# Router logits of an attention + mixture-of-experts kernel: token strips turned by VectorE instead of TensorE transposes, and two products instead of eight for the counts

## The chip, the cores and the metric

One core of one Trainium2 chip. The metric is the device time of one execution in microseconds, the median of 3 runs; lower is better.

## What is computed

Sigmoid attention on 8 batches x 12 heads x 448 tokens x 64, its output read as 3584 tokens x 768, and a mixture of experts on top of it, in which a token takes part only when its skip score is positive, and then with one expert:

```python
scores = scale * np.matmul(q, k.transpose(0, 1, 3, 2)) - np.log(S)
x = np.matmul(1.0 / (1.0 + np.exp(-scores)), v)      # rearranged to (3584, 768)
do_compute = x @ w_skip > 0
logits = x[do_compute] @ w_gate                        # 8 experts
e_idx = argmax(logits);  gate_w = softmax(logits)[e_idx]
y[e_idx == e] = gate_w * (relu(x @ w1[e]) @ w2[e])     # w1: 768x1024, w2: 1024x768
out = x.copy();  out[do_compute] = x + y
```

## The kernel before, in words

**Attention** runs as 48 steps `n`, one for each batch `b` and pair of heads `hp` (6 pairs in a batch), in an order written out by hand (`tc.manual_schedule`, the loop at line 692). A step has four parts `c` of keys (parts 0 to 2 with 448 queries, part 3 with 224). For each part TensorE makes scores (`scores`, L223, tile `s`), ScalarE takes the sigmoid (L243, tile `at`), and TensorE multiplies with the values two parts later (`values`, L251, tile `pa`). Keys and queries are loaded by SP two steps ahead, partly copied by GpSimd (L173) and turned by VectorE (L191). The finished rows of a pair are kept in `xt` (L689 on ScalarE, L261 on VectorE), turned (L266, tile `y`) and stored.

All tiles of scores share two PSUM slots, which alternate:

```python
def new_s(name):
    turn[0] ^= 1
    return ps_s.tile([P, 2, 512], F32, tag=f"s{turn[0]}", name=name)
```

`new_t`, from which the tiles of the router come, takes the next of the same two slots during attention. A tile in a slot is free when its last reader is done, and the scores two places later wait for that.

**Routing of batch b-1 lies inside the steps of batch b.** `xt` holds the 768 features on partitions, in six blocks `i` of 128, and the 448 tokens on columns.

- hp 0, part 3: `logits` (L291) multiplies each block with 32 weight columns (8 gates, the skip vector, zeros) in one of four column groups of TensorE: blocks 0 to 3 with all 448 tokens, one per group, blocks 4 and 5 in two halves of 224 tokens. The four groups hold partial sums. `keep_logits` (L302) copies all of it, 128x448, out of PSUM on VectorE (tile `lt`).
- hp 1, part 2: `turn_logits` turns `lt` by four TensorE transposes of 112 tokens (L308, tile `pg`, a slot of its own) and VectorE adds the four partial sums (L312, tile `lg`). `route` then finds the expert: `mx`, `d`, `first`, `fm`, `hot`, and `hb`, a one for the chosen expert of each token (L322 to L356).
- hp 2: `gates` (L376 to L382), and in part 3 `route_count`: each token's place in its expert's list is a count of earlier tokens of that expert. With the token's chunk of 112 on columns and the token within it on partitions, this takes one product with a triangle (L388), three with ones for the chunks before (L390) and four that sum all chunks for the running `base` (L398), all into `pc`, again in a slot. VectorE reads it (L406 to L420: `pos`, `base`, `sel`, `idx`).
- Four indirect DMAs on GpSimd (L425) put the records into the experts' lists.

The last batch does this after the loop (lines 840 to 886), between the products of the first expert block (`gemm1`, L527; `gemm2`, L555): `logits` with `parts=4`, where blocks 4 and 5 go in four pieces of 112 tokens. From step 22 on SP also loads weights of the first expert (tile `wr`), which VectorE and GpSimd split (L496, L497). After that a loop over blocks of tokens (L1558) does the rest; where few rows are left (`few`, L1403), its products have 32 weight columns and 128 moving columns in four column groups (L1409).

In the profile every product of float32 operands stands as two records, one for each half of its weights.

Of the kernel before, what the change touches and what calls it, by code (L numbers as in the profile page):

```python
# [10 lines left out]
F32 = mybir.dt.float32  # L11
F32R = mybir.dt.float32r
BF16 = mybir.dt.bfloat16
I32 = mybir.dt.int32
# [5 lines left out]
P = 128  # L20
# [3 lines left out]
def kernel(  # L24
# [62 lines left out]
    ones = const.tile([CP, P], BF16, name="ones")  # L87
    nc.vector.memset(ones, 1.0)

# [3 lines left out]
    nc.gpsimd.iota(tok_i, pattern=[[CP, NC]], base=0, channel_multiplier=1)  # L93
# [185 lines left out]
    def col(c):  # L279

        return slice(c * CP, (c + 1) * CP)
# [17 lines left out]

    def keep_logits(b, pl):  # L300
        lt = io.tile([P, S], F32, tag="wr", name=f"lt_{b}", bufs=WB)
        nc.vector.tensor_copy(lt, pl[:, :S])  # L302
        return lt

    def turn_logits(b, lt):
        pg = new_t(f"pg_{b}")
        for c in range(NC):
            nc.tensor.transpose(  # L308
                pg[:CP, c * P : (c + 1) * P], lt[:, col(c)], ident
            )  # L310
        lg = sm.tile([CP, NC, NE + 1], F32, tag="lg", name=f"lg_{b}", bufs=1)
        nc.vector.tensor_reduce(  # L312
            lg,
            pg[:CP, :].rearrange("p (c g e) -> p c e g", c=NC, g=4)[:, :, : NE + 1, :],
            axis=AX.X,
            op=ALU.add,
        )
        return lg

    def route(b, lg):  # L320
        mx = sm.tile([CP, NC], F32, tag="mx", name=f"mx_{b}", bufs=1)
        nc.vector.tensor_reduce(mx, lg[:, :, :NE], axis=AX.X, op=ALU.max)  # L322
        rec = sm.tile([CP, NC, REC], F32, tag="rec", name=f"rec_{b}")
        nc.gpsimd.memset(rec, 0.0)
        nc.gpsimd.tensor_scalar(
            rec[:, :, 1], tok[:CP], float(b * S), None, op0=ALU.add
        )
        d = sm.tile([CP, NC, NE], F32, tag="d", name=f"d_{b}", bufs=1)
# [3 lines left out]
            mx.unsqueeze(2).to_broadcast([CP, NC, NE]),  # L332
# [3 lines left out]
        first = sm.tile([CP, NC, NE], F32, tag="first", name=f"first_{b}", bufs=1)  # L336
# [4 lines left out]
            desc[:CP].unsqueeze(1).to_broadcast([CP, NC, NE]),  # L341
# [3 lines left out]
        fm = sm.tile([CP, NC], F32, tag="fm", name=f"fm_{b}", bufs=1)  # L345
        nc.vector.tensor_reduce(fm, first, axis=AX.X, op=ALU.max)
        hot = sm.tile([CP, NC, NE], F32, tag="hot", name=f"hot_{b}", bufs=1)
# [3 lines left out]
            fm.unsqueeze(2).to_broadcast([CP, NC, NE]),  # L351
# [3 lines left out]
        hb = sm.tile([CP, NC, NE], BF16, tag="hb", name=f"hb_{b}", bufs=1)  # L355
        nc.vector.scalar_tensor_tensor(  # L356
            hb,
            lg[:, :, NE : NE + 1].to_broadcast([CP, NC, NE]),
# [4 lines left out]
        )  # L363
        return rec, hb, d

    def weigh_route(b, rt):

        sg = sm.tile([CP, NC, NE], F32, tag="sg", name=f"sg_{b}", bufs=1)
# [3 lines left out]
    def gates(b, rt):  # L372
        rec, sg = rt[0], sgs[b]

        om = sm.tile([CP, NC, NE], F32, tag="om", name=f"om_{b}", bufs=1)
# [3 lines left out]
        sume = sm.tile([CP, NC], F32, tag="sume", name=f"sume_{b}", bufs=1)  # L379
# [4 lines left out]
    def route_count(b, rec, hb):  # L384
# [1206 lines left out]
```

## Time and profile before

| | us |
|---|---|
| median of 3 runs (lowest, highest) | 521.59 (521.33, 522.76) |
| the profiled execution | 520.3 |
| its span, first to last instruction | 518.5 |
| TensorE busy in the span | 505.6 (98%) |
| VectorE, ScalarE, GpSimd busy | 294.2, 279.2, 239.8 |
| attention (up to the last scores) | about 279 of the span |
| granted TensorE clock, mean | 0.993 |

The profiled execution is 1.3 us under the median, and 1.8 us of it lie outside the span. The records of TensorE overlap in time (four groups work at once), so what a piece of its work costs is read from where the next piece starts, not from the length of its records.

### The profile page before, as it was taken

How to read it: one execution, taken by the hardware profiler on the slowest of the kernel's cores; microseconds unless marked ns; L12 is line 12 of the kernel's file. 1: busy time of each engine (PE TensorE's matmuls, PEld its weight loads, DVE VectorE, ACT ScalarE, POOL GpSimd, SP SyncE). 2: the span in 40 equal slices, each digit the busy share in tenths (PEclk: the TensorE clock that was granted, in tenths of full speed). 3: DMA queues.
4: the chain of work that ended last, by engine and by line, in shares of the span. 5: the costliest groups of instructions: out<-in, count | busy, mean ns of one | idle time of the engine just before them, and what ended most of it. 6: DMA issues, size and time to landing. Idle time of an engine off the chain costs nothing.

```text
span 518.5 us, 15420 instructions
## 1 busy us (share of the span) xinstructions
PE 505.6 (98%) x5037; PEld 342.8 (66%) x5038; DVE 294.2 (57%) x696; ACT 279.2 (54%) x481; POOL 239.8 (46%) x355
## 2 busy tenths in 40 slices
PE   8999999999999999999999999999999999999991
PEld 6885555555545555555455889957769797979790
DVE  4546856658578678775695862681222332349522
ACT  5776786767767766677676212761122323258321
POOL 4523454443457676765675402332321434344634
PEclk9999999999999999999999999999999999999997
DMA  8998877897999999989975106949395879796943
GB/s 206 207 250 190 186 170 156 174 174 173 202 194 234 223 206 216 200 192 228 195 157 118 20 32 199 383 124 363 105 350 191 269 286 296 262 329 243 348 177 47
DMA packets 142081, 107.22 MB, mean 207 GB/s; under 512 B 99163, under 2 KB 114523, under 8 KB 142032
## 3 DMA queue, kind: packets, MB, share of 16 engines
q1 hardware_dynamic: 133792, 96.11, 71.3%
q0 software_dynamic: 4032, 8.51, 6.7%
q10 hardware_dynamic: 4208, 1.95, 1.5%
q8 instruction: 30, 0.49, 0.4%
q14 instruction: 19, 0.16, 0.1%
HBM read 98.49 MB, written 17.56 MB: 224 GB/s over the span
## 4 chain that ended last, share of the span: by engine, by line
PE 93%; DVE 2%; DMA 1%; issue 1%; POOL 1%; SPq 1%; ACT 0%; POOLq 0%; ACTq 0%; DVEq 0%
PE s L223 24%; PE pa L251 23%; PE ph L527 11%; PE py L555 11%; PE b_ph L527 3%; PE b_py L555 3%; PE ph L1409 3%; PE py L1409 2%; PE py L1478 2%; PE ph L1478 2%; PE pxt L503 2%; PE pl L291 2%; PE pht L541 1%; PE pg L308 1%; DMA kq<-in_k_dram 1%
## 5 line engine op out<-in xcount | busy, mean ns | idle before, releaser
L243 ACT ACTIVATE at<-s,bias 128x896 f32<-128x896 f32 (+1 forms) x191 | 174.0, 914 | 79.6 <-PE s L223 68.8
L251 PE MATMUL pa<-at,v 64*64 64x448 f32 (+1 forms) x1536 | 168.3, 489 | 0.0
L223 PE MATMUL s<-x 64*64 64x448 f32 (+1 forms) x1504 | 166.7, 496 | 0.4 <-DVE sel L418 0.4
L173 POOL COPY kq<-kq 32x896 f32<-32x896 f32 (+1 forms) x96 | 87.9, 915 | 96.2 <-DMA kq<-in_q_dram 55.8
L223 PEld LDWEIGHTS s<-x 64*64 64x64 f32 x1504 | 82.6, 191 | 47.9 <-issue 25.4
L251 PEld LDWEIGHTS pa<-at,v 64*64 64x64 f32 x1536 | 65.8, 133 | 54.6 <-issue 45.6
L191 DVE STREAM_TRANSPOSE x<-kq 128x448 f32<-128x448 f32 x94 | 80.7, 931 | 4.7 <-POOL kq L173 4.7
L261 DVE TENSOR_TENSOR xt<-xt,pa 128x448 f32<-128x448 f32 x48 | 29.7, 619 | 50.8 <-ACT xt L689 50.8
L425 POOL DMA_INDIRECT lst<-rec,idx x32 | 31.6, 988 | 16.3 <-issue 5.3
L497 POOL TENSOR_TENSOR wl<-wr,wh 128x384 fp32r<-128x384 f32 (+1 forms) x28 | 31.5, 1136 | 11.1 <-DVE wh L496 7.6
L266 DVE STREAM_TRANSPOSE y<-xt 128x448 f32<-128x448 f32 x48 | 31.0, 645 | 7.8 <-DMA out_dram<-y 6.3
L547 DVE TENSOR_TENSOR hl<-pht,hh 128x512 fp32r<-128x512 f32 x14 | 9.7, 689 | 41.4 <-ACT hh L546 41.4
L536 ACT ACTIVATE hs<-ph 128x512 f32<-128x512 f32 x14 | 8.4, 599 | 42.1 <-PE ph L527 26.3
L585 POOL DMA_INDIRECT out_dram<-ys,rp x15 | 22.8, 1519 | 16.3 <-POOLq L1558 8.4
L555 PE MATMUL py<-wh,hh 128*128 128x384 f32 x112 | 29.8, 347 | 0.0
L555 PE MATMUL py<-wh,hl 128*128 128x384 f32 x112 | 28.8, 338 | 0.0
L555 PE MATMUL py<-wl,hh 128*128 128x384 f32 x112 | 28.7, 337 | 0.0
L513 DVE TENSOR_TENSOR xl<-pxt,xh 128x384 fp32r<-128x384 f32 x30 | 15.3, 551 | 20.8 <-ACT xf L1108 20.3
L527 PE MATMUL ph<-wl,xh 128*128 128x512 f32 x84 | 26.3, 400 | 0.0
L689 ACT ACTIVATE xt<-pa 128x448 f32<-128x448 f32 x48 | 25.7, 536 | 0.8 <-PE pa L251 0.8
L527 PE MATMUL ph<-wh,xh 128*128 128x512 f32 x84 | 25.4, 399 | 0.0
L527 PE MATMUL ph<-wh,xl 128*128 128x512 f32 x84 | 24.1, 391 | 0.0
(268 smaller groups left out, 657.0 us busy)
## 6 DMA issues: line engine op xcount, KB each, us to landing
raw<-in_moe_w_dram SPq DMA_DIRECT2D x48, 768.0 KB, 9.5
v<-in_v_dram SPq DMA_DIRECT2D x48, 256.0 KB
out_dram<-y SPq DMA_DIRECT2D x192, 56.0 KB
raw<-in_moe_w_dram SPq DMA_DIRECT2D x7, 1536.0 KB
kq<-in_k_dram SPq DMA_DIRECT2D x46, 224.0 KB
kq<-in_q_dram SPq DMA_DIRECT2D x46, 224.0 KB
wr<-in_moe_w_dram SPq DMA_DIRECT2D x12, 256.0 KB
wr<-in_moe_w_dram SPq DMA_DIRECT2D x16, 192.0 KB
```

Of the source, the lines that this page charges most:

```text
L173: nc.gpsimd.tensor_copy(a[BT:, :, :, :BT], a[:BT, :, :, BT:])
L191: nc.vector.transpose(xs[:, n].rearrange("p (r j) -> p j r", j=NJ), t.rearrange("p (j d) -> p j d", d=D)[:, :, :BT],)
L223: nc.tensor.matmul(sc[m * D : (m + 1) * D, j, : qs.stop - qs.start], xs[r, 0, first::NR7], xs[r, 1, qs], start=True, stop=True,)
L243: nc.scalar.activation(at[:, :, :n], sc[:, :, :n], AF.Sigmoid, bias=bias, scale=SCALE)
L251: nc.tensor.matmul(pa[j * D : (j + 1) * D, r, qs], vt[rs, j, r + c if c < 3 else 3 * (1 - r), :], at[rs, j, : qs.stop - qs.start], start=( ...
L261: nc.vector.tensor_tensor(x, x, pa[:, 1, :S], op=ALU.add)
L266: nc.vector.transpose(y, xts[b][:, hp, :])
L425: put = nc.gpsimd.indirect_dma_start(out=lst[:, :], out_offset=bass.IndirectOffsetOnAxis(ap=idx[:, c : c + 1], axis=0), in_=rec[:, c, :], ...
L497: nc.gpsimd.tensor_tensor(lo, r, hi, op=ALU.subtract)
L527: nc.tensor.matmul(ph[h], a[:, j * P : (j + 1) * P], w[j][h], start=(n == 0), stop=(n == len(t) - 1),)
L555: last = nc.tensor.matmul(half_y(py, o), a[h][:, js], w[j][:, o * H2 : (o + 1) * H2], start=(j == 0 and n == 0), stop=(j == NK2 - 1 and n ...
L1409: nc.tensor.matmul(dst[g * SM : (g + 1) * SM, :n], a, w, start=(j == 0), stop=(j == most - 1), tile_position=(0, g * SM),)
```

## The change

- The logits of a batch are made in four strips of 112 tokens: strip `g` in column group `g`, all six blocks summed in PSUM. 24 products of 112 columns take the place of 8 of 448 or 224, and no partial sums are left over.
- VectorE clears the 16 columns behind the strips and turns 128x128 out of PSUM in 32x32 blocks straight into SBUF. The TensorE transposes, their slot `pg` and the adding reduction are gone. Tokens now lie on all 128 partitions (32 of each strip, 16 lanes of the last chunk empty), and `route`, `gates` and `idx` work on 128 partitions.
- Two VectorE additions make running sums of `hb` over the chunks (`cum`), and two products, with ones and with the triangle, take the place of eight.
- `tok_i` is made by four small iotas later on GpSimd, and three constant tiles are cleared at the start.

```diff
-    ones = const.tile([CP, P], BF16, name="ones")
+    ones = const.tile([P, P], BF16, name="ones")
     nc.vector.memset(ones, 1.0)
+    hbp = const.tile([P, NC + 2, NE], BF16, name="hbp")
+    hbs = const.tile([P, NC + 2, NE], BF16, name="hbs")
+    cum = const.tile([P, NC + 1, NE], BF16, name="cum")
...
-    def logits(pl, ks, xt, parts):
+    def logits(pl, ks, xt):
         for i in ks:
-            n = 1 if i < 4 else parts
-            for h in range(n):
-                g = (i * n + h) % 4
-                cols = slice(h * S // n, (h + 1) * S // n)
+            for g in range(4):
                 nc.tensor.matmul(
-                    pl[32 * g : 32 * (g + 1), cols],
+                    pl[32 * g : 32 * (g + 1), :CP],
                     wcat[:, i, :],
-                    xt[:, i, cols],
-                    start=(i < 4),
-                    stop=(i >= NK1 - 4 // parts),
+                    xt[:, i, g * CP : (g + 1) * CP],
+                    start=(i == 0),
+                    stop=(i == NK1 - 1),
                     tile_position=(0, 32 * g),
                 )
-    def keep_logits(b, pl):
+    def turn_logits(b, pl):
         lt = io.tile([P, S], F32, tag="wr", name=f"lt_{b}", bufs=WB)
-        nc.vector.tensor_copy(lt, pl[:, :S])
-        return lt
-    def turn_logits(b, lt):
-        pg = new_t(f"pg_{b}")
-        for c in range(NC):
-            nc.tensor.transpose(
-                pg[:CP, c * P : (c + 1) * P], lt[:, col(c)], ident
-            )
...
-        nc.vector.tensor_reduce(
...
+        nc.vector.memset(pl[:, CP:P], 0.0)
+        nc.vector.transpose(lt[:, :P], pl[:, :P])
+        return lt[:, :P].rearrange("p (c e) -> p c e", c=NC)
...
-        hb = sm.tile([CP, NC, NE], BF16, tag="hb", name=f"hb_{b}", bufs=1)
+        hb = hbp[:, 2:]
...
+        nc.vector.tensor_tensor(hbs[:, 2:], hb, hbp[:, 1 : NC + 1], op=ALU.add)
+        nc.vector.tensor_tensor(cum[:, 1:], hbs[:, 2:], hbs[:, :NC], op=ALU.add)
...
-        nc.tensor.matmul(pc[:CP, :n], tri[:CP, :CP], hb.rearrange("p c e -> p (c e)"), start=True, stop=False)
-        for s in range(1, NC):
-            nc.tensor.matmul(
-                pc[:CP, s * NE : n],
-                ones[:, :CP],
...
-        for s in range(NC):
-            nc.tensor.matmul(
-                pc[:, n : n + NE],
-                ones,
-                hb[:, s, :],
...
+        nc.tensor.matmul(pc[:, : n + NE], ones, cum.rearrange("p c e -> p (c e)"), start=True, stop=False)
+        nc.tensor.matmul(pc[:, :n], tri, hb.rearrange("p c e -> p (c e)"), start=False, stop=True)
...
-                logits(pl, range(NK1), xts[pb], 2)
-            if c == 2 and hp == 1 and b > 0:
-                lg = turn_logits(pb, lts[pb])
+                logits(pl, range(NK1), xts[pb])
...
-                    rts[pb] = route(pb, lg)
+                    rts[pb] = route(pb, lts[pb])
...
-                lts[pb] = keep_logits(pb, pl)
+                lts[pb] = turn_logits(pb, pl)
```

How it moves the work. First TensorE in batch 1, from hp 0, part 3 to hp 1, part 3: `pl` are the logits, `pg` the transposes, `s` scores and `pa` values; before, and then with the change.

```order
L291 MATMUL pl_650<-xt_220,wcat 32x448 x4
L291 MATMUL pl_650<-xt_220,wcat 32x224 x4
L223 MATMUL s_1_0_671<-x_1_598 64x448 x4
L251 MATMUL pa_0_634<-at_0_2_627,v_0_490 64x448 x4
L223 MATMUL s_1_1_684<-x_1_598 64x448 x4
L251 MATMUL pa_0_634<-at_0_3_639,v_0_490 64x224 x4
L223 MATMUL s_1_2_696<-x_1_598 64x448 x4
L251 MATMUL pa_1_702<-at_1_0_670,v_0_490 64x448 x4
L308 MATMUL pg_707<-ident,lt_663 112x128 x4
L223 MATMUL s_1_3_730<-x_1_598 64x224 x4
```

```order
L289 MATMUL pl_659<-xt_229,wcat 32x112 x24
L229 MATMUL s_1_0_697<-x_1_607 64x448 x4
L257 MATMUL pa_0_643<-at_0_2_636,v_0_499 64x448 x4
L229 MATMUL s_1_1_710<-x_1_607 64x448 x4
L257 MATMUL pa_0_643<-at_0_3_648,v_0_499 64x224 x4
L229 MATMUL s_1_2_722<-x_1_607 64x448 x4
L257 MATMUL pa_1_728<-at_1_0_696,v_0_499 64x448 x4
L229 MATMUL s_1_3_750<-x_1_607 64x224 x4
```

The logits are 24 short products instead of 8, and nothing stands between the values of part 2 and the scores of part 3 any more; the rest keeps its order.

Then VectorE over the same steps, from the reading of `pl` (`lt`) to `hb` and what follows it; `x` and `y` are the turned operands and rows of attention.

```order
L302 COPY lt_663<-pl_650 128x448
L191 STREAM_TRANSPOSE x_2_677<-kq_2_524 128x14x32 x2
L312 TENSOR_REDUCE lg_712<-pg_707 112x36
L322 TENSOR_REDUCE mx_714<-lg_712 112x4
L329 TENSOR_TENSOR d_719<-lg_712,mx_714 112x32
L337 SCALAR_TENSOR_TENSOR first_721<-d_719,desc 112x32
L346 TENSOR_REDUCE fm_723<-first_721 112x4
L348 TENSOR_TENSOR hot_725<-first_721,fm_723 112x32
L356 SCALAR_TENSOR_TENSOR hb_727<-lg_712,hot_725 112x32
L261 TENSOR_TENSOR xt_586<-xt_586,pa_0_634 128x448
```

```order
L301 MEMSET pl_659 128x16
L302 STREAM_TRANSPOSE lt_688<-pl_659 128x128
L197 STREAM_TRANSPOSE x_2_703<-kq_2_533 128x14x32 x2
L307 TENSOR_REDUCE mx_733<-lt_688 128x4
L314 TENSOR_TENSOR d_738<-lt_688,mx_733 128x32
L322 SCALAR_TENSOR_TENSOR first_740<-d_738,desc 128x32
L331 TENSOR_REDUCE fm_742<-first_740 128x4
L333 TENSOR_TENSOR hot_744<-first_740,fm_742 128x32
L341 SCALAR_TENSOR_TENSOR hbp<-lt_688,hot_744 128x32
L350 TENSOR_TENSOR hbs<-hbp 128x32
L351 TENSOR_TENSOR cum<-hbs 128x32
L267 TENSOR_TENSOR xt_595<-xt_595,pa_0_643 128x448
```

The copy becomes a clearing and a transpose at the same place, the reduction that read `pg` is gone, and the two additions stand behind `hb`.

Last, TensorE in hp 2, part 3 of batch 1, around the counts `pc`:

```order
L388 LDWEIGHTS tri
L388 MATMUL pc_813<-hb_727,tri 112x32
L390 LDWEIGHTS ones
L390 MATMUL pc_813<-hb_727,ones 112x24
L390 LDWEIGHTS ones
L390 MATMUL pc_813<-hb_727,ones 112x16
L390 LDWEIGHTS ones
L390 MATMUL pc_813<-hb_727,ones 112x8
L398 LDWEIGHTS ones
L398 MATMUL pc_813<-hb_727,ones 128x8
```

```order
L257 MATMUL pa_2_809<-at_2_1_783,v_2_625 64x448 x4
L376 LDWEIGHTS ones
L376 MATMUL pc_833<-cum,ones 128x40
L377 LDWEIGHTS tri
L377 MATMUL pc_833<-hbp,tri 128x32
L229 MATMUL s_3_0_854<-x_3_777 64x448 x4
```

Of the eight products before, five are shown, each with its weight load; three more of the last kind follow. Two are left.

## Rows read from the trace of the kernel before

**Rows 1.** The page of the profile, part 1: busy time of each engine, its share of the span, its instructions.

```profile
PE 505.6 (98%) x5037; PEld 342.8 (66%) x5038; DVE 294.2 (57%) x696; ACT 279.2 (54%) x481; POOL 239.8 (46%) x355
```

**Rows 2.** Stretches of attention by window, each from one batch's logits to the next (the first from the start of the second step): length, busy us and records of PE, PEld, DVE, ACT and POOL, granted clock, mean busy share of the DMA engines, GB/s. Shown are the first stretch, the fifth and the sixth.

```profile
10.64:42.95 32.31, 32.31 (x392) 25.75 (x385) 16.82 (x23) 24.93 (x31) 13.53 (x16) 1.00 1.01 231
...
146.47:180.97 34.50, 34.50 (x416) 18.11 (x412) 25.86 (x50) 24.50 (x32) 22.95 (x24) 1.00 1.01 219
180.97:216.16 35.19, 34.80 (x417) 19.45 (x413) 27.38 (x51) 24.50 (x32) 25.67 (x29) 1.00 1.01 214
```

**Rows 3.** The timeline of TensorE in batch 1: start in us, length, line, tiles, form, records merged.

```profile
42.95 1.34 PE L291 MATMUL pl<-xt,wcat 128*32 128x448 f32 x16
44.22 1.04 PE L223 MATMUL s<-x 64*64 64x448 f32 x8
...
45.83 0.93 PE L223 MATMUL s<-x 64*64 64x448 f32 x8
...
47.71 0.93 PE L251 MATMUL pa<-at,v 64*64 64x448 f32 x8
48.58 0.65 PE L308 MATMUL pg<-ident,lt 128*112 128x128 f32 x4
49.15 0.67 PE L223 MATMUL s<-x 64*64 64x224 f32 x8
49.64 0.93 PE L251 MATMUL pa<-at,v 64*64 64x448 f32 x8
...
54.53 0.56 PE L223 MATMUL s<-x 64*64 64x224 f32 x8
54.91 0.93 PE L251 MATMUL pa<-at,v 64*64 64x448 f32 x8
55.77 0.22 PE L388 MATMUL pc<-hb,tri 112*112 112x32 bf16 x1
55.84 0.30 PE L390 MATMUL pc<-hb,ones 112*112 112x24 bf16 x3
56.00 0.24 PE L398 MATMUL pc<-hb,ones 112*128 112x8 bf16 x4
56.17 1.04 PE L223 MATMUL s<-x 64*64 64x448 f32 x8
57.03 0.93 PE L251 MATMUL pa<-at,v 64*64 64x448 f32 x8
57.79 0.93 PE L223 MATMUL s<-x 64*64 64x448 f32 x8
```

**Rows 4.** The timeline of the last batch's routing, on PE, PEld (the weight loads) and, in one row, VectorE.

```profile
281.03 1.15 PE L291 MATMUL pl_last<-xt,wcat 128*32 128x448 f32 x16
...
281.81 0.13 PEld L291 LDWEIGHTS pl_last<-xt,wcat 128*32 128x32 f32 x4 [0.25 <-issue]
...
282.11 0.87 PE L503 MATMUL b_px<-ident,x 128*128 128x128 f32 x6
...
282.92 0.40 PE L291 MATMUL pl_last<-xt,wcat 128*32 128x112 f32 x8
...
283.29 1.67 PE L527 MATMUL b_ph<-wh,b 128*128 128x512 f32 x6
...
284.80 0.86 PE L527 MATMUL b_ph<-wl,b 128*128 128x512 f32 x3
...
285.85 0.94 PE L527 MATMUL b_ph<-wl,b 128*128 128x512 f32 x3
...
286.13 0.31 DVE L312 TENSOR_REDUCE lg<-pg 112x36 f32<-112x144 f32 x1 [0.76 <-PE pg L308]
...
286.63 1.55 PE L527 MATMUL b_ph<-wh,b 128*128 128x512 f32 x6
...
288.02 0.18 PE L388 MATMUL pc<-hb,tri 112*112 112x32 bf16 x1
...
288.30 1.62 PE L527 MATMUL b_ph<-wh,b 128*128 128x512 f32 x6
```

**Rows 5.** The timeline of TensorE in a block with few rows: 12 sets of four products, 32 weight columns and 128 moving columns each, and what follows them.

```profile
401.36 2.83 PE L1409 MATMUL ph<-raw,xf 128*32 128x128 f32 x96
404.12 0.33 PE L1430 MATMUL pht<-ident,hs 128*128 128x128 f32 x1
```

**Rows 6.** Waits during attention: who waited for whom, us in total, times, longest.

```profile
POOL kq L173 <- DMA kq<-in_q_dram: 55.8, 19, 8.0
...
DVE lg L312 <- PE pg L308: 15.5, 7, 2.6
```

**Rows 7.** The timeline of VectorE and GpSimd: the first turn of a key tile at the start, and in batch 1 the copy of the logits, GpSimd's copies in hp 2, and the last reader but one of `pc`.

```profile
4.44 0.62 DVE L646 STREAM_TRANSPOSE x_first<-kq_first 128x128 f32<-128x128 f32 x2 [3.01 <-ACT kq_first L622]
...
44.95 0.58 DVE L302 COPY lt<-pl 128x448 f32<-128x448 f32 x1
...
54.49 3.87 POOL L173 COPY kq<-kq 32x896 f32<-32x896 f32 x4 [8.95 <-DVE om L377]
...
57.47 0.18 DVE L418 TENSOR_REDUCE sel<-pos 112x4 f32<-112x32 f32 x1
```

**Rows 8.** The timeline of TensorE in batch 5, behind the counts: values, and the scores that come after them.

```profile
195.06 0.93 PE L251 MATMUL pa<-at,v 64*64 64x448 f32 x8
196.38 1.04 PE L223 MATMUL s<-x 64*64 64x448 f32 x8 [0.39 <-DVE sel L418]
```

More of the change, by code (lines that the diff above doesn't have):

```diff
@@ L85 @@
     nc.vector.memset(wcat, 0.0)
-    ones = const.tile([CP, P], BF16, name="ones")
+    ones = const.tile([P, P], BF16, name="ones")
     nc.vector.memset(ones, 1.0)
+    hbp = const.tile([P, NC + 2, NE], BF16, name="hbp")
+    hbs = const.tile([P, NC + 2, NE], BF16, name="hbs")
+    cum = const.tile([P, NC + 1, NE], BF16, name="cum")
+    nc.vector.memset(hbp, 0.0)
+    nc.vector.memset(hbs, 0.0)
+    nc.vector.memset(cum, 0.0)
     ramp_i = const.tile([P, NE], I32, name="ramp_i")
@@ L92 @@
     tok_i = const.tile([P, NC], I32, name="tok_i")
-    nc.gpsimd.iota(tok_i, pattern=[[CP, NC]], base=0, channel_multiplier=1)
     slot_i = const.tile([P, 1], I32, name="slot_i")
@@ L325, in route @@
         nc.gpsimd.tensor_scalar(
-            rec[:, :, 1], tok[:CP], float(b * S), None, op0=ALU.add
+            rec[:, :, 1], tok, float(b * S), None, op0=ALU.add
         )
-        d = sm.tile([CP, NC, NE], F32, tag="d", name=f"d_{b}", bufs=1)
+        d = sm.tile([P, NC, NE], F32, tag="d", name=f"d_{b}", bufs=1)
         nc.vector.tensor_tensor(
@@ L331, in route @@
             lg[:, :, :NE],
-            mx.unsqueeze(2).to_broadcast([CP, NC, NE]),
+            mx.unsqueeze(2).to_broadcast([P, NC, NE]),
             op=ALU.subtract,
         )
-        first = sm.tile([CP, NC, NE], F32, tag="first", name=f"first_{b}", bufs=1)
+        first = sm.tile([P, NC, NE], F32, tag="first", name=f"first_{b}", bufs=1)
         nc.vector.scalar_tensor_tensor(
@@ L340, in route @@
             0.0,
-            desc[:CP].unsqueeze(1).to_broadcast([CP, NC, NE]),
+            desc.unsqueeze(1).to_broadcast([P, NC, NE]),
             op0=ALU.is_ge,
@@ L416, in route_count @@
         nc.vector.tensor_tensor(base, base, pc[:, n : n + NE], op=ALU.add)
-        sel = sm.tile([CP, NC], F32, tag="sel", name=f"sel_{b}", bufs=1)
+        sel = sm.tile([P, NC], F32, tag="sel", name=f"sel_{b}", bufs=1)
         nc.vector.tensor_reduce(sel, pos, axis=AX.X, op=ALU.add)
-        idx = sm.tile([CP, NC], I32, tag="idx", name=f"idx_{b}")
+        idx = sm.tile([P, NC], I32, tag="idx", name=f"idx_{b}")
         nc.vector.tensor_scalar(idx, sel, OOB, None, op0=ALU.add)
@@ L623 @@
         nc.gpsimd.tensor_copy(*first_part(n, 0))
+    for g in range(4):
+        nc.gpsimd.iota(
+            tok_i[g * BT : (g + 1) * BT], pattern=[[BT, NC]], base=g * CP, channel_multiplier=1
+        )
     vs = {0: load_v(0, 0, 2)}
@@ L842 @@
     pl = new_t("pl_last")
-    logits(pl, range(NK1 - 1), xt, 4)
+    logits(pl, range(NK1 - 1), xt)
     keep_values(*done)
@@ L855 @@
         split_x(h, px, xh0, xl0)
-    logits(pl, [NK1 - 1], xt, 4)
-    lt = keep_logits(lb, pl)
+    logits(pl, [NK1 - 1], xt)
+    lg = turn_logits(lb, pl)
     store_rows(lb, NPAIR - 1, turn_rows(lb, NPAIR - 1))
@@ L860 @@
     py = new_s("b0_py")
+    rec, hb, _ = rt = route(lb, lg)
     gemm1(0, range(9), xh0, xl0, ph)
-    rec, hb, _ = rt = route(lb, turn_logits(lb, lt))
     weigh_route(lb, rt)
```

40 lines of the change are left out of this document (12 added, 28 removed).

## The prediction

> **What bounds the kernel now.** I read the page first: TensorE is busy in 98% of the span, VectorE in 57% [rows 1]. Then attention by windows: between two batches' logits TensorE is busy the whole time, at the full granted clock of 1.00, also in the first stretch, which has no routing in it [rows 2]. So attention is paced by TensorE's own work, and a piece costs what lies between its start and the next one's. In batch 1 a plain piece of scores or values takes 0.76 us (57.03 to 57.79) and scores of part 3 take 0.38 (54.53 to 54.91) [rows 3]. Against these the routing stands out. The logits take 1.27 (42.95 to 44.22). The transposes take 0.57 (48.58 to 49.15); moreover the values ahead of them take 0.87, not 0.76, and the scores behind them 0.49, not 0.38: 0.11 at each change of the array's shape. The counts take 0.40 (55.77 to 56.17), with the same 0.11 on either side (54.91 to 55.77, and 56.17 to 57.03) [rows 3]. The reader should see that TensorE never pauses at them: what is taken out there moves everything behind it.
>
> **The change, part by part.**
>
> *Transposes (out).* 0.57 and two edges of 0.11 make 0.79 us for each batch in the loop; there are seven (VectorE waited for them seven times [rows 6]). The values ahead and the scores behind have one shape, so the edges go as well: 7 x 0.79 = 5.5 us. The slot that `pg` took goes too, so no scores wait longer for a slot than now.
>
> *Counts (eight products to two).* In the old run the first product is followed after 0.07, the next three take 0.16 and the last four 0.17 [rows 3]. Two products then cost between 0.09 (two of the last kind) and 0.24 (the first, and all of the last four). I take the middle, 0.17, as none of the rows has just this pair. It saves 0.23 a batch, 0.16 to 0.31; the edges stay. 7 x 0.23 = 1.6 us.
>
> *Logits (24 short products).* The four groups work side by side, and the columns stay 2688 in all. The price of columns comes from two rows: a set of 448 and one of 224 columns take 1.27 [rows 3], in the last batch one of 448 and one of 112 take 1.08 (281.03 to 282.11) [rows 4]. The 112 columns between them cost 0.19, that is 0.095 for each of the two records that a product has. Twelve such records per group are 1.14, and 1.27 less that leaves 0.13 for filling and emptying, once. Six sets of 112 are twelve records again: 1.27, no change. The ends: 1.14, if nothing is lost at the edges; and above, the pace of a block with few rows, where 24 records per group of 128 columns take 2.76 (401.36 to 404.12) [rows 5], less 0.13 and by 24 that is 0.11 each, so 1.45 if short records cannot go faster than that. From 0.13 less to 0.18 more a batch; I take 0, as the 112 columns were measured at just this size.
>
> There are three times as many weight loads. In the last batch four loads take 0.13 us, inside the 1.15 of the products around them [rows 4]. A rule speaks against this part: the Trainium skill ("TensorE: Matmul & The Clock Gate", in Part 3, section "The mechanism") has weight loads overlap running products only when they go to another row group, and all strips use the same rows. By it, each of the six sets would wait for its own loads, and the sum would come out as in the second rival below; the rows of the block with few rows, all in one row group, don't bear it out so far.
>
> *VectorE.* The copy of 0.58 [rows 7] gives way to clearing 16 columns and turning 128 out of PSUM. No row shows such a turn; it lies between nothing and the 0.58 of the copy of 448 columns, and I take half of that. The slot is wanted by the scores at 45.83 [rows 3], 0.30 after the copy ended, so it is hidden; without that cover the pair would cost at most 0.58 a batch. The reduction goes and two additions come. They are covered by the time in which VectorE waited for the transposes, 15.5 us in seven batches [rows 6]. Where `cum` is read, TensorE is a whole step later.
>
> *Last batch.* Six products, the transposes and their edges take 1.83 (284.80 to 286.63), six products alone 1.39 (286.63 to 288.02): 0.44 less. The counts take 0.28 (288.02 to 288.30), and by the same ratio 0.12 after: 0.16 less. The logits are ten records and two, as before (1.08, and 0.37 from 282.92 to 283.29): no change. Together 0.6. VectorE must not be late for the counts: it saves the 0.76 that it waited and the reduction of 0.31 [rows 4], and two additions, each no longer than that reduction, take back 0.62 at most.
>
> *What is late next.* The scores two pieces behind the counts take the slot of `pc`, and VectorE must have read it. In batch 1 it is done at 57.65 [rows 7], and they start at 57.79 [rows 3]: 0.14 to spare, and TensorE comes 0.23 earlier, so a wait of 0.09. In batch 5 they already wait: 1.32 from the values ahead to them (195.06 to 196.38) instead of 0.76 [rows 8]; there the 0.23 is lost too. For the two I add 0.3; the ends are nothing (VectorE comes earlier, too) and 7 x 0.23 = 1.6.
>
> *Start.* VectorE idles 3.01 us there [rows 7], which hides the three clearings. Four iotas come ahead of GpSimd's copies for the second step; I take nothing, up to 0.5 if they delay it.
>
> **Sum.** 5.5 + 1.6 + 0.6 - 0.3 = 7.4. The profiled execution took 520.3, so 512.9; the median shown is 521.59, 1.3 more, so I forecast **514.2**. With all low ends, 7 x (0.79 + 0.31 + 0.13) + 0.6 = 9.2 gives 512.4; with all high ends, 7 x (0.79 + 0.16 - 0.18) + 0.6 - 1.6 - 0.5 = 3.9 gives 517.7.
>
> **The rivals.**
>
> *DMA becomes the pace in the busy batches.* In the fifth and sixth stretch the DMA engines' busy share is 1.01, at 219 and 214 GB/s [rows 2]. A batch that is 1.0 us shorter needs 219 x 34.5 / 33.5 = 226 GB/s. For it: GpSimd already waits 55.8 us for keys and queries [rows 6], so loads come in no earlier than needed. Against it: the first stretch ran at 231 GB/s with TensorE busy in all of its 32.31 us [rows 2]. If three batches (those with the expert's weights) keep their time, 3 x 1.0 comes back: 517.2. Chance 0.12.
>
> *The short products don't hide their loads.* Then each set of 112 costs what the single set in the last batch costs, 0.37 (282.92 to 283.29) [rows 4]: six make 2.2, 0.95 more than now. 7 x 0.95 and 0.8 in the last batch eat 7.4: 521.6, no change. Against it stands the pace of 96 records in 2.76 [rows 5]. Chance 0.05.
>
> *VectorE's reading of the counts becomes the bound: slower.* Place: the scores two pieces behind the counts, which wait for the slot. GpSimd's four copies (3.87 us) already lie among VectorE's short instructions there [rows 7], and the new timing may push more of VectorE's chain behind them. It decides from a wait of 1.0 us in each batch on, when it eats what a batch gains; if VectorE came one pair of copies (1.9 us) later in all seven, 7 x (1.9 + 0.23 - 0.14) = 13.9 would come on, 528. For it: batch 5 loses 0.56 so today [rows 8]; against it: the other batch shown is in time. Chance 0.02.
>
> **How the numbers follow.** My forecast, with a range of its own of 512.4 to 516.5 (not all high ends come at once), has 0.77; 0.04 is for gains cut in ways I don't see, still faster. A measurement of this kernel tells about 0.3% from no change, 1.6 us. Faster by more: 0.77 + 0.12 + 0.04 = 0.93; within it 0.05; slower 0.02. The range of 512.4 to 517.4 takes in the forecast and the case of DMA; what is left out is the unhidden loads, the slower case and the tails.
>
> **What would show it right or wrong.** In the changed profile a batch from logits to logits should take about 33.5 us, not 34.5, with TensorE still busy throughout; logits 1.27 (2.2 speaks for the second rival, 1.45 for the pace of the few rows); counts 0.17; values and scores of hp 1 back to back at 0.76 and 0.38. If the busy stretches stay at 34.5 with GpSimd or VectorE waiting on loads, it is DMA. If the scores behind the counts wait for `sel` in most batches, it is the third rival. The blocks after attention should keep their durations and only start earlier.

## The result and the profile after

The changed kernel takes 526.17 us (median of 6 runs, 525.68 to 527.33), the kernel before 521.46 beside it on the same chip: a ratio of 1.0091, with an interval of 1.0075 to 1.0107. It is slower, where I forecast 514.2 and gave slower a chance of 0.02. The profiled execution has a span of 525.3 us, 518.5 before: 6.8 more.

Read in the order of the prediction, attention first. The page of the kernel after, part 1, answers to [rows 1]: TensorE is busy 2.2 us less, in a span that is 6.8 longer, so its share has fallen by two points.

```profile
PE 503.4 (96%) x5205; PEld 353.4 (67%) x5206; DVE 290.7 (55%) x715; ACT 278.5 (53%) x481; POOL 239.8 (46%) x358
```

The timeline of TensorE in batch 1 of the kernel after, which answers to [rows 3]:

```profile
42.84 1.36 PE L289 MATMUL pl<-xt,wcat 128*32 128x112 f32 x48
44.12 1.04 PE L229 MATMUL s<-x 64*64 64x448 f32 x8
...
47.62 0.93 PE L257 MATMUL pa<-at,v 64*64 64x448 f32 x8
48.37 0.56 PE L229 MATMUL s<-x 64*64 64x224 f32 x8
48.75 0.93 PE L257 MATMUL pa<-at,v 64*64 64x448 f32 x8
...
54.88 0.19 PE L376 MATMUL pc<-cum,ones 128*128 128x40 bf16 x1
54.92 0.18 PE L377 MATMUL pc<-hbp,tri 128*128 128x32 bf16 x1
55.02 1.04 PE L229 MATMUL s<-x 64*64 64x448 f32 x8
```

The logits take 1.28 (42.84 to 44.12). Values and scores follow each other at 0.75 and 0.38 where the transposes were. The counts take 0.14 (54.88 to 55.02). VectorE's new pair in the same batch, clearing and turning, is short:

```profile
44.80 0.07 DVE L301 MEMSET pl<- 128x16 f32 x1
44.91 0.32 DVE L302 STREAM_TRANSPOSE lt<-pl 128x128 f32<-128x128 f32 x1
```

Attention by windows from one batch's logits to the next, batches 1 and 5 to 7, with the columns of [rows 2] (batch 4 is the fifth stretch there, batch 5 the sixth):

```profile
42.84:76.31 33.47, 33.47 (x437) 18.03 (x434) 22.01 (x46) 24.36 (x32) 15.26 (x19) 1.00 0.84 181
...
177.61:211.27 33.66, 33.66 (x438) 18.36 (x435) 24.35 (x52) 24.45 (x32) 23.38 (x25) 1.00 0.97 208
211.27:247.30 36.03, 34.29 (x439) 19.79 (x435) 23.60 (x52) 24.48 (x32) 23.94 (x27) 1.00 0.97 203
247.30:277.82 30.52, 30.08 (x391) 15.96 (x387) 20.75 (x48) 20.49 (x27) 21.95 (x27) 1.00 0.75 155
```

The first four batches keep the forecast's 33.5 within 0.3. Then the gain stops: batches 5 to 7, the late batches from here on, take 100.2 us together (177.61 to 277.82), and they took 100.1 before (180.97 to 281.03). Batch 5 still gains 1.5 and batch 6 loses as much. In batch 6 VectorE waits 2.28 us for a load of the first expert's weights (`wr`), its next row (`xt`) is late by that, and TensorE waits 1.20 us for the row (what stands in brackets is idle time and what ended it):

```profile
227.24 1.06 DVE L469 CAST wh<-wr 128x384 fp32r<-128x384 f32 x1 [2.28 <-DMA wr<-in_moe_w_dram]
...
228.88 0.61 PE L257 MATMUL pa<-at,v 64*64 64x448 f32 x4 [1.20 <-DVE xt L267]
```

Still, the last logits start 3.2 us earlier, and the loop over the expert blocks is entered 4.0 us earlier (TensorE's first branch at 315.31, before at 319.26).

There the kernel loses. The timeline of TensorE in the kernel after, at the entry of that loop and at its second round:

```profile
317.35 0.51 PE L528 MATMUL b_py<-wh,b 128*128 128x384 f32 x2
322.78 0.77 PE L500 MATMUL ph<-wh,xh 128*128 128x512 f32 x1 [4.92 <-issue]
323.34 0.63 PE L500 MATMUL ph<-wl,xh 128*128 128x512 f32 x1
...
331.48 0.39 PE L500 MATMUL ph<-wh,xl 128*128 128x512 f32 x1
...
346.07 5.46 PE L1453 MATMUL ph<-raw,xf 128*64 128x512 f32 x24 [1.93 <-issue]
```

TensorE stands still for 4.92 us and again for 1.93, and nothing that the profile counts as a wait ended either gap ("issue"). What it did shows in the branches of one line. They stand in the code that chooses an arm, which is the code for one kind of block. A row gives their count, then the shortest, the median and the longest in ns. First the kernel before, then the kernel after, and after it again in the window of 340 to 345 us alone.

```profile
L1553 PEldq COMPARE_BRANCH  x8: 73/194/293, 320.9 to 473.0; - x8
```

```profile
L1528 PEldq COMPARE_BRANCH  x8: 73/196/5729, 316.9 to 479.8; - x8
...
L1528 PEldq COMPARE_BRANCH  x1: 3288/3288/3288, 340.8 to 340.8; - x1
```

The jump into the first block's arm takes 5.73 us (before 0.24), and the jump out of it 3.29 (before 0.29). The gaps are shorter than the jumps, because TensorE still has products in its queue when its sequencer jumps (at 316.9; the last two products start at 317.35 and after). In the window of the first jump, 316.8 to 322.7 us, the DMA queues of the kernel after show two transfers of instructions among the weights:

```profile
q10 hardware_dynamic: 494, 1.47, 63.8%
q1 hardware_dynamic: 272, 0.56, 30.0%
q8 instruction: 1, 0.02, 1.1%
q14 instruction: 1, 0.01, 0.5%
```

Queue q8 brings TensorE's code: a run below with 256 more TensorE instructions (e2) has one more packet on it, and as many on q14. Asked in short windows, the transfer on q8 starts 3.3 us into this jump (between 320.1 and 320.2) and 1.0 us into the second (between 341.75 and 341.85).

Windows over the gap and the slow part of the first gemm behind it, in the kernel after (granted clock third from the end):

```profile
317.86:322.78 4.92, 0.00 (x1) 0.03 (x1) 1.14 (x2) 0.00 (x0) 1.04 (x1) 0.93 1.04 379
322.78:330.00 7.22, 7.22 (x19) 5.69 (x20) 0.00 (x0) 0.00 (x0) 0.00 (x0) 0.57 1.02 380
```

After the gap the granted clock is 0.57 on average over 7.2 us: most of that stretch ran at the lower of the two levels, 1.2 GHz, and a product takes 0.43 us (323.34 to 323.77) in place of 0.23 (331.48 to 331.71). The ledger, at the starts of TensorE's products, in us: it would have been 3.8 ahead at the loop's first product (317.86 for 321.64). It loses 4.9 in the first gap, 2.9 in the gemm behind it (11.7 from 322.78 to 334.48, before 8.85), and 1.9 in the second gap, so it is 6.0 behind at the second round's first product (346.07, before 340.10). Another 0.1 in that round and 0.8 in the later long rounds make the 6.8 at the end.

### The profile page after: what moved, and what is told of

The parts are those of the page before. It is cut to its first block, busy times and chain, and to the rows that moved or that the text cites. A ratio compares the mean times of both kernels' runs of the same rounds, so it can differ in the third digit from the quotient of the medians.

```text
span 525.3 us, 15806 instructions
## 1 busy us (share of the span) xinstructions
PE 503.4 (96%) x5205; PEld 353.4 (67%) x5206; DVE 290.7 (55%) x715; ACT 278.5 (53%) x481; POOL 239.8 (46%) x358
## 4 chain that ended last, share of the span: by engine, by line
PE 80%; DMA 7%; issue 3%; DVE 3%; SPq 3%; POOL 2%; ACT 1%; ACTq 0%; POOLq 0%; DVEq 0%
PE pa L257 18%; PE s L229 18%; PE ph L500 12%; PE py L528 11%; PE b_ph L500 3%; PE b_py L528 3%; PE ph L1384 3%; PE py L1384 2%; PE ph L1453 2%; PE py L1453 2%; PE pxt L476 2%; DMA kq<-in_q_dram 2%; DMA wr<-in_moe_w_dram 1%; PE pl L289 1%; PE pht L514 1%
## 5 line engine op out<-in xcount | busy, mean ns | idle before, releaser
L229 PEld LDWEIGHTS s<-x 64*64 64x64 f32 x1504 | 85.8, 191 | 47.7 <-issue 18.3
L257 PEld LDWEIGHTS pa<-at,v 64*64 64x64 f32 x1536 | 69.7, 133 | 52.0 <-issue 38.1
L500 PE MATMUL ph<-wh,xh 128*128 128x512 f32 x84 | 27.1, 418 | 4.9 <-issue 4.9
L500 PE MATMUL ph<-wl,xh 128*128 128x512 f32 x84 | 27.6, 416 | 0.0
L500 PE MATMUL ph<-wh,xl 128*128 128x512 f32 x84 | 25.4, 406 | 0.0
```

The lines of the kernel that those rows point to most:

```text
L229: nc.tensor.matmul(sc[m * D : (m + 1) * D, j, : qs.stop - qs.start], xs[r, 0, first::NR7], xs[r, 1, qs], start=True, stop=True,)
L257: nc.tensor.matmul(pa[j * D : (j + 1) * D, r, qs], vt[rs, j, r + c if c < 3 else 3 * (1 - r), :], at[rs, j, : qs.stop - qs.start], start=( ...
L500: nc.tensor.matmul(ph[h], a[:, j * P : (j + 1) * P], w[j][h], start=(n == 0), stop=(n == len(t) - 1),)
```

## Theories

**Theory 1, code.** TensorE's instructions come by transfers of 16384 bytes (the page's queue of instructions: 32 packets, 0.52 MB). One transfer brings 256 instructions, as e2's one packet more shows. The change makes TensorE's program 350 instructions longer ahead of the loop, counted in the programs as built: the longer logits add 496, the transposes and counts take away 160, and 14 waits come. By that count the loop's start moved from place 251 to place 89 within a block of 256. The arm of the first block and the loop's end moved with it, each across a block's edge, and TensorE jumps to code that has not been fetched. **Theory 2, the work.** The same time is lost because weights, rows and lists now start 4 us earlier and collide. Beside these, what holds the late batches was to be found.

## The experiments

All ratios are to the kernel before, run on the same chip in turn.

**The code put back where it was** (e1):

```
-    keep_busy(9)
+    for _ in range(46):
+        nc.tensor.matmul(idle[:32, 0, :8], ident[:, :32], ident[:, :8], start=True, stop=True)
+    keep_busy(3)
```

> The changed kernel, with 40 more f32 products at its start (46 of 8 columns and 3 wide ones in place of the 9 wide ones; TensorE has nothing else to do there), which is 160 TensorE instructions of 64 bytes: the code of the expert loop then stands against the 16384-byte blocks in which instructions are fetched as it does in the kernel before (loop start at 249 of 256 instructions in place of 89; before: 251). Theory 1 (code): the two jumps of 5.73 and 3.29 us fall to about 0.25 us each, the first gemm in the loop runs at the higher clock again (8.9 us in place of 11.7), and the time is 526.2 - 10.7 + 0 to 1.5 for the added products = 515.5 to 517. Theory 2 (the work): the 10.7 us come from weight loads and rows that start 3.9 us earlier and collide, whatever the place of the code: 526 to 527.5.

520.17 us, ratio 0.9958 (0.9946 to 0.9970). The longest of the eight branches at the choice is back at 0.30 us:

```profile
L1530 PEldq COMPARE_BRANCH  x8: 73/196/302, 319.6 to 472.5; - x8
```

The jumps and the clock behaved as theory 1 has it, and what they cost is won back whole: from the loop's entry to the first product of its second round e1 takes 21.0 us, the kernel after 30.8 and the kernel before 20.8. The time missed its range by 3 us. Of these, 0.9 lies in my 10.7: it took in the later long rounds, and e1 has them as long as the kernel after (18.66). The added products cost more than I allowed: the first logits start 3.4 us later (46.21 for 42.84), and the loop is still entered 2.6 later.

**One whole block more** (e2): the same edit with 70 for 46.

> The control of the same kind: the changed kernel with 64 more f32 products at the start (70 narrow and 3 wide), 256 instructions, one whole block of 16384 bytes, so that the loop's code stands in its blocks as it does in the changed kernel. Theory 1 (code): both jumps stay at 3 to 6 us, 526 to 528.5. A theory by which any work at the start (a warmer clock, a later start of the batches) is what helps expects the gain of the 40 products here too, 515.5 to 518. Theory 2: 526 to 528.5.

533.77 us, ratio 1.0233 (1.0203 to 1.0264), 5 us above the range: the added products cost 5.0 us at the first logits, which I had not counted. (Its four runs lie between 530.8 and 535.1; the profiled one is the fastest.) The long jump stays, so it isn't the added work that helped in e1:

```profile
L1530 PEldq COMPARE_BRANCH  x8: 73/198/6130, 320.2 to 482.7; - x8
```

**The kernel before, with its code where the change has it** (e3): the same edit in the kernel before with 30 for 46.

> The kernel before, with 24 more f32 products at the start (30 narrow and 3 wide), 96 instructions, which puts the loop's code where the changed kernel has it (91 of 256 for the loop's start in place of 251; after: 89); nothing of the change is in it. Theory 1 (code): the two jumps that took 0.24 and 0.29 us take 3 to 6 us each, TensorE idles for some 7 us in sum, and its clock falls after the first: 521.5 + 7 to 11 = 528.5 to 532.5. Theory 2 (the work): 521.5 to 523.

532.95 us, ratio 1.0220 (1.0195 to 1.0244), half a us above the range. Nothing of the change is in it, and its added products cost nothing at the first logits (42.97 for 42.95). Both long jumps are there, in all branches and in the window of 340 to 349 us:

```profile
L1555 PEldq COMPARE_BRANCH  x8: 73/200/5695, 322.5 to 483.2; - x8
...
L1555 PEldq COMPARE_BRANCH  x1: 3167/3167/3167, 345.1 to 345.1; - x1
```

Theory 2 falls, theory 1 holds: the loss comes and goes with the place of the code, on either kernel.

**What a fetch costs** (e4, e11). In the changed kernel, with its code where the change puts it, first one weight load more waits for the last product ahead of the loop, then all seven do, on one queue:

```
     for n in range(4):
         load = load_w1(n % 2, n // 2, nx)
-        if n == 1:
+        if n == 0:
             tc.add_manual_dep(
...
-        load_w2(g, nx if g < 2 else nx_act, nc.sync if g < 2 else nc.scalar)
+        load_w2(g, nx)
```

The last pair of lines is e11's alone.

> The changed kernel, code places as they are, but the first of the four weight loads of the loop's first block waits for the last product ahead of the loop too, as the other three do. Theory 1a (the code block that the first jump needs queues behind the weight loads): the first jump falls from 5.73 us to 1 to 3.5 us, and the time to 521 to 525 if nothing waits for the later weights. Theory 1b (the fetch itself takes 5 us, whatever else is under way): the jump keeps 5 to 6 us, 526 to 527. Theory 2: fewer bytes in collision, some us less, with both jumps as long as before.

> The changed kernel, code not placed, with all seven weight loads of the loop's first block behind the last product ahead of the loop and on one queue, the one that ScalarE issued too. Theory 1a (of the first jump's 5.7 to 5.8 us, 3.2 are the fetch itself, as at the second jump, and the rest is queueing behind weight loads under way): 3.2 to 4 us at the first jump now. Theory 1b (the first fetch is long for another reason): 5.5 to 6 us still. The time is not the point here: 523 to 528.

e4: 528.12 us, ratio 1.0106 (1.0081 to 1.0131), jumps of 5.82 and 3.21 us. Weights were still under way at the first (2.00 MB in 318.8 to 324.7), so it left the queueing open. e11: 527.41 us, ratio 1.0090 (1.0055 to 1.0126). Its two jumps, in the windows of 310 to 330 and 330 to 345 us:

```profile
L1528 PEldq COMPARE_BRANCH  x1: 3500/3500/3500, 319.6 to 319.6; - x1
...
L1528 PEldq COMPARE_BRANCH  x1: 5152/5152/5152, 338.5 to 338.5; - x1
```

The lengths have changed places. At the first jump the DMA engines are now little used (busy share 0.13 and 0.30 in the two us from 320), and it takes 3.5. At the second the late loads fill them (1.07 from 338 to 340), and it takes 5.2. The transfers on q8 say where the difference lies. In e11 the transfer starts 0.6 us into the first jump and 2.8 into the second; in the kernel after it was 3.3 and 1.0. From the start of the transfer to the end of the jump it takes 2.3 to 2.9 us all four times. Theory 1a holds: a fetch costs 3.2 to 3.5 us by itself, and some 2 more before the transfer starts in queues full of weights. The wait was only moved, so the time is the changed kernel's.

**The code placed without added work** (e5): a directive that starts the first product at a given instruction of a block, with a jump over the gap.

```
+    nc.tensor.addr_align(256, offset=219, max_nops=0)
     keep_busy(9)
```

> The changed kernel with its code moved and no instruction added: one alignment directive ahead of the first product puts that product at instruction 219 of a 16384-byte block, and the expert loop's start then at about 48, near where the kernel before has it; the gap is jumped over while TensorE waits for its first data. Theory 1 (code): both jumps at 0.2 to 0.3 us, and none of the 3.4 us that the added products cost in the kernel with the added products: 526.2 - 10.7 = 515.5, 514.5 to 516.5. A theory by which the added products helped in another way (a warmer clock, a later start) expects 525 to 527. What the forecast had without the loss at the loop, 514.2, is missed by the waits on transfers in the last two batches (1.3 us).

520.35 us, ratio 0.9948 (0.9929 to 0.9968); the upper end of the range was 516.5. Both jumps are at 0.29 us or less, but the branch ahead of them now takes 1.73. It ends 2.4 us after a transfer on q8 started (317.0), as the long jumps do:

```profile
L1523 PEldq COMPARE_BRANCH  x14: 74/83/1727, 317.6 to 498.5; - x14
```

That is worth 0.9 us: from the loop's entry to the second round's first product it takes 21.8 us (before 20.8). Besides, the late batches took 100.7 us.

**The parts alone** (e6, e7), code placed by the same directive. e6 is the kernel before with `cum` and the two products of the change; e7 is the changed kernel with the eight products of before.

> The kernel before with the counts of the change alone (running sums, two products for eight), logits as before, and the code placed by the same directive. By the forecast's term, 7 x 0.23 us: 521.5 - 1.6 = 519.9 (519 to 520.7). A theory by which the short products cost nothing beside the gemms and value products expects 521.5.

> The changed kernel with the eight count products of before on the new layout (128 partitions), so that the logits in strips and the turn by VectorE are the only change; the code placed by the same directive. By the forecast's term, 7 x 0.79 us less the 1.5 to 3 us that waits on transfers took back in the last two batches: 521.5 - 5.5 + 1.5 to 3 = 517.5 to 519. Without those waits 516.

e6: 524.43 us, ratio 1.0031 (1.0017 to 1.0045). Its second and third batch take 34.27 and 34.29, 0.23 less than before, as the term has it; but a branch waits 1.6 us as in e5, the late batches take 101.6, and the sum is a loss where a gain of 1.6 was expected. e7: 520.08 us, ratio 0.9947 (0.9928 to 0.9967), which beside 521.5 is 518.7 and within the range; it is also the ratio of both parts together, so in the total the counts can't be seen. That the total fits is in part luck. Its second and third batch take 34.18 each, 0.32 less than before and not 0.79: in batch 2 the logits take 1.85 us, and in batch 3 scores wait 0.6 for VectorE's turn (`lt`). Without these two the batches would be at 33.6.

**Bytes, addresses, buffers** (e8, e9, e10). e8 brings half of each weight load's columns:

```
...
-            src[ds(ev, 1), j * P : (j + 1) * P, h * n : (h + 1) * n].rearrange(
+            src[ds(ev, 1), j * P : (j + 1) * P, h * n : h * n + n // 2].rearrange(
...
+        r = r.unsqueeze(1).to_broadcast([P, 2, r.shape[1]])
```

> The changed kernel with its code placed, and in the last batches of the attention half the bytes of the first expert's weight loads: each load brings half of its columns, and the two engines that split it read them twice, so their work stays and the results of the first expert are not the reference's. Theory A (in the last two batches the transfers set the pace: 36.0 us for one batch where 33.7 is TensorE's own, and waits of 3.0 and 2.8 us): batches at 33.5 to 33.8 throughout, 2 to 3.5 us less than the placed kernel, 512 to 513.5. Theory B (something else holds the batches): 515 to 516 as the placed kernel.

518.35 us, ratio 0.9920 (0.9901 to 0.9938), 2.0 less than e5. But the late batches took 99.8, where two batches of 33.5 and a last one 1.0 shorter than before would be some 96.4 (an estimate). It is inconclusive.

e9 and e10 place the code with offset 251 and add a spare constant of 224 bytes; e10 also gives every second pair of heads row buffers of its own:

```
+    const.tile([P, 56], F32, name="spare")
...
-        y = wk.tile([P, S], F32, tag="y", name=f"y_{b}_{hp}")
+        y = (sm if hp % 2 else wk).tile([P, S], F32, tag="y", name=f"y_{b}_{hp}")
```

> The changed kernel with its code placed once more, the loop's start 32 instructions further into its block (first product at 251), and a spare constant of 224 bytes per partition, so that the first expert's weights and all that is allocated behind them lie 512 bytes from where the kernel before has them in place of 288. Theory of the two small losses in the placed kernel: the jump that took 1.73 us there falls to 0.3 to 0.5 us (its code block is asked for earlier), and the 512-column gemm products, 0.233 us each there and 0.227 before, go back to 0.227 (address of the weights), which is worth 0.13 to 0.16 us in each of the loop's seven long iterations; together 2.2 us less than the placed kernel, a ratio to before of 0.9915 (0.990 to 0.993), some 517 beside 521.5. If the products' pace has nothing to do with the address, they stay at 0.233 and the ratio is 0.9935.

> The kernel above with four buffers in place of two for the rows that VectorE turns and the store engines send out (odd pairs of heads get two of their own). Theory C (in the last two batches VectorE waits for a store to leave one of two buffers, 4.0 and 6.9 us in sum in the placed kernel, and what is behind it on VectorE holds TensorE up): those waits go, and the last batches fall from 34.5 and 32.2 us towards 33.6 and 31: 1 to 2.5 us less than the kernel above. Theory A (the transfers' bandwidth sets the pace there): the waits move to the loads of q, k and the weights, and the time stays within 0.7 us.

e9: 520.35 us, ratio 0.9957 (0.9935 to 0.9979), where 0.9915 was expected. Branch (0.39 us) and products (0.227) came out as expected, but the first scores start at 7.42 us, not 5.84. TensorE waits there for VectorE's turn of the first keys and queries, and that waits for their load:

```profile
6.14 0.57 ACT L596 ACTIVATE kq_first<-kq_first 32x448 f32<-32x448 f32 x1 [1.53 <-DMA kq_first<-in_q_dram]
...
7.42 1.04 PE L218 MATMUL s<-x_first 64*64 64x224 f32 x8 [1.67 <-DVE x_first L628]
```

The first product stands at 251 here, five instructions in front of a block's end, and a block of code is fetched 3.1 us into the run, among these first loads. That the fetch delays them is not shown: e10, with the same place, is as late (7.49), but e12 below has such a fetch too (3.6) and is not.

e10: 521.82 us, ratio 0.9988 (0.9962 to 1.0014). The waits of the late batches, first in e9, then in e10:

```profile
POOL kq L180 <- DMA kq<-in_q_dram: 9.9, 6, 3.0
DVE y L273 <- DMA out_dram<-y: 9.2, 4, 3.3
```

```profile
POOL kq L180 <- DMA kq<-in_q_dram: 9.8, 7, 2.8
```

More buffers take away the 9.2 us on stores and no time: theory C falls. GpSimd's wait for its loads is as long as before.

**Placed once more, and without the weight loads** (e12, e13). e12 is e9 with offset 235. e13 is e12 with one weight load in place of 28, and offset 238:

```
...
+        if not only:
+            only.append(sm.tile([P, H1], F32, tag="only", name="only", bufs=1))
+            nc.sync.dma_start(
+                only[0],
...
+        r = only[0][:, :n]
```

> The changed kernel with the spare constant of 224 bytes, and the first product at instruction 235 of its block: the loop's start then stands 16 instructions further than in the first placed kernel (its second jump took 1.73 us there), and 21 instructions fit in front of the first block's end (5 did in the kernel before this one, whose first scores came 1.5 us late). Expected if the code's place and the weights' address are what was left: first scores at 5.8 to 6.0 us, no jump over 0.6 us, gemm products at 0.227 us, and a ratio to before of 0.9905 (0.988 to 0.9935). If one of these is not what holds it, 0.994 to 0.996 again.

> The kernel above, but of the first expert's 28 weight loads only the first is made, and the engines split that one piece 28 times: their work stays, and the results of the first expert are not the reference's. Theory A (transfers set the pace of the last three batches): from the fifth batch's logits to the last one's 96.5 to 98.5 us, where the kernels with the loads have 98.8 to 102.7, and 2 to 4 us less than the kernel above. Theory D (a chain of waits on stores and list writes, whatever the weights bring): 99 to 102 us there, and within 1 us of the kernel above.

e12: 519.92 us, ratio 0.9957 (0.9934 to 0.9979). First scores at 5.82, no branch above 0.39, every round of the loop within 0.1 of the kernel before: the three named causes are gone, and the ratio is not the 0.9905 I expected. What is left is the late batches, 101.9 us. e13: 520.36 us, ratio 0.9959 (0.9942 to 0.9976). Windows of batches 5 and 6, in e12 and in e13:

```profile
178.21:213.66 35.45, 34.11 (x438) 19.98 (x435) 25.46 (x52) 24.47 (x32) 24.65 (x26) 1.00 1.02 212
213.66:247.86 34.20, 33.77 (x438) 18.70 (x435) 25.20 (x52) 24.48 (x32) 24.39 (x28) 1.00 1.01 211
```

```profile
180.00:213.69 33.69, 33.69 (x439) 18.77 (x435) 25.16 (x53) 24.49 (x32) 22.85 (x25) 1.00 0.84 172
213.69:247.31 33.62, 33.62 (x439) 19.54 (x435) 24.79 (x52) 24.48 (x32) 23.95 (x27) 1.00 0.85 172
```

With the loads gone the busy share of the DMA engines falls to 0.85, and these two batches run at TensorE's own pace, busy throughout. The late batches take 98.1, as theory A has it. One execution each is little, though: in e2, with all its loads, the same two batches take 33.48 and 33.47, and the late batches 98.8. Nor did e13's total move. TensorE's last product ends at 505.1, 2.6 earlier than in e12 (507.7), and the span is the same, 518.4 and 518.3: the 2.6 are lost behind that product. Between 512 us and the end two small blocks of instructions are fetched (TensorE's are 16384 bytes, these 8192):

```profile
q14 instruction: 2, 0.02, 0.6%
```

In e12 none is fetched there. That leaving out 27 loads moved another engine's code across an edge, as the change did TensorE's, would fit; it was not tried.

**Loads moved into the last batch** (e14 on e12, with the alignment's offset at 234; e15 on the kernel before):

```
-    how_many = (1, 1, 1, 1, 1, 2) * 4
+    how_many = (1, 1, 1, 1, 0) * 3 + (1, 1, 1, 1, 1) + (2, 2, 2, 3, 2)
```

> The changed kernel with code and addresses placed as in the last one, and the 28 weight loads of the first expert spread otherwise: 17 in the 20 steps up to the last batch (23 there before) and 11 in the last batch's first five steps (5 before), where transfers have room. Theory A (transfers pace the three last batches): 98 to 100 us from the fifth batch's logits to the last one's (101.9 in the placed kernel), 1.5 to 3.5 us less in the end, a ratio to before of 0.989 to 0.993. Theory D (a chain that has nothing to do with these loads, or the last batch taking in what the others gain): 100.5 to 103 us there, ratio 0.994 to 0.998.

> The kernel before with the weight loads spread in the same way and nothing else. Theory A: its TensorE has 34.5 us of work in a batch, and the loads hold it only by 0.7 us in one batch, so it gains 0 to 1 us at most: ratio 0.998 to 1.001. If the new spread alone is what helps, whatever TensorE has to do, it gains as much as the changed kernel, 0.993 to 0.996.

e14: 519.68 us, ratio 0.9940 (0.9918 to 0.9963). Batch 5 falls to 33.5, from 35.45 in e12, and batch 7 grows to 33.25, from 32.3: 101.4 for the late batches, which is within theory D's numbers. e15: 525.24 us, ratio 1.0060 (1.0047 to 1.0073), worse than either theory had it: its batches 5 and 6 take 34.8 and 34.5, and batch 7 takes 31.6 in place of 30.4. In these two runs, moving loads only moved the place where time is lost.

## Why the prediction was wrong

- **Transposes: right.** Pieces are back to back at 0.75 and 0.38. **Counts: right**, 0.14 for the 0.17 that I took; e6 has 0.23 less per batch. **Logits: right**, 1.28 for 1.27. The second rival and the rule named beside it fall for this shape: 48 records with a load each go by in 1.28 us. What I had no step for: in many of these kernels the logits of one batch, mostly the second, take up to 1.9 us.
- **VectorE: right**, 0.32 for the turn. **Last batch: right**, from its first gemm to that of the next block 18.5 us (280.09 to 298.55), 19.2 before; 0.7 for the 0.6 of the term. **Slot of `pc`: right in size.** In the kernel after, the scores two pieces behind the counts come 0.17 and 0.14 late in batches 2 and 3 (0.92 and 0.89 for 0.75), when VectorE has only just read `pc`; I had put 0.3 on batches 1 and 5.
- **The rival on DMA was the likely case, and I gave it 0.12.** I took the first stretch, which ran at 231 GB/s without a pause, as proof that the transfers had room. Its loads may have been ahead of it, which no run tested; in the late batches the waits for loads are in the traces. The three batches kept their time in sum, as the rival had it, and at the loop the kernel was 4.0 ahead, 517.5 beside 521.5: the rival's 517.2 was the time to name for what TensorE does in attention. The best kernels here with all loads have 0.994 to 0.996, some 518.4 to 519.3 beside 521.5, since the late batches are at times longer than before. That bandwidth alone holds those batches, not the order of the transfers as well, isn't shown: e8 halved the bytes and freed little, e13 freed them and e2 nearly did with all loads, and all kernels with all loads lie between 98.8 and 102.7 us there.
- **The step that failed: "The blocks after attention should keep their durations and only start earlier."** It counted what TensorE executes, not where the code that it has to fetch lies. Tripling the logits' products cost nothing where they run (1.28 for 1.27) and moved the loop's code behind the edge of a fetch block. The two jumps grew by 5.5 and 3.0 us and left TensorE idle for 4.9 and 1.9, and the lower clock behind the first gap made up most of 2.9 more. No rival spoke of it. The trace of before had only hints: a queue of instructions, and branches of 0.2 to 0.5 us.

The kernels with placed code beat both: e5, e12 and e14 by 0.4 to 0.6% against the kernel before, and by 1.3 to 1.5% against the change as it was made, by the ratios of each to the kernel before.

## What to carry to other kernels

Count what an edit adds to an engine's program, not only to its time: where a long straight stretch is followed by a loop with jumps, the code's place in its fetch blocks belongs to the change, and a run with the code moved (or aligned) tells whether a slowdown is the idea's or the address's. A gap of "issue" ahead of an instruction behind a jump, a long branch on that engine's queue, and a transfer of instructions in the same window are one finding. And where transfers are busy all the time, an engine's saved time is to be followed stretch by stretch: in the late batches here, which wait for loads, it did not count.

## What the runs showed of the hardware

- A jump to code that isn't there costs 3.2 to 3.5 us with few transfers under way, 5.2 to 6.1 among weight loads (e2, e3, e4, e11 and the kernel after). What differs is when the transfer of 16384 bytes starts: 0.6 to 1.0 us into the jump, or 2.8 to 3.3 (e11 and the kernel after).
- After 4.9 us without a product the granted clock fell to the lower level, 1.2 GHz, for some 6 us of products in the kernel after (0.57 on average over 7.2 us). In e3, after a gap of 4.8, the lower level lasted a shorter time (0.64 over 4.8 us). After the 2.7 us gap in e11 the clock stayed at 1.00 over the whole gemm (323.24 to 332.15).
- The place of a tile in memory goes with a product's pace, a little. From 345 to 500 us, the same 72 products of 512 columns, first in the kernel after, whose weights by the programs lie 288 bytes from where they lay before, then in e12, where they lie 512 bytes from it (the kernel before has e12's mean):

```profile
L500 PE MATMUL ph<-wh,xh 128*128 128x512 f32 x72 | 21.0, 404 | 0.0
```

```profile
L501 PE MATMUL ph<-wh,xh 128*128 128x512 f32 x72 | 20.7, 400 | 0.0
```

The long rounds of the loop take 18.66 and 17.64 us in the one and 18.50 and 17.50 in the other: some 0.9 us in a run. All nine kernels with the three small constants of the counts and without the spare one take 404 ns, whatever the place of their code, and the other eight 400 or 401. Only these places were tried.
